# A new task order for the first attention tiles: first score ahead of the second head's similarities, first q and k in two transfers, block copies on ScalarE

## The chip, the cores and the metric

The kernel runs on one core of one Trainium2 chip. The metric is the device time of one execution in microseconds (us). A core has TensorE (PE; its weight loads are listed apart as PEld), VectorE (DVE), ScalarE (ACT), GpSimd (POOL) and SyncE (SP), which issues every transfer of this kernel.

## The reference

The kernel computes a clustered attention, then two feed-forward layers. With B = 2, H = 8 heads, S = 768 positions, D = 64 and 16 centroids per head:

```
q_assign = argmax(normalize(q) . normalize(centroids))       # and the same for k
scores   = where(q_assign == k_assign, q k^T / sqrt(D), -1e9)
attn     = softmax(scores) v                                 # 16 (batch, head) pairs
x        = attn, heads side by side                          # 1536 x 512
h        = max(x w1, x w2, x w3);  x2 = h w_out              # width 768
P        = Sinkhorn of exp(x2 w_gate), 8 rounds              # 1536 x 8
out      = sum over 8 experts e of P[:, e] * (relu(x2 w1[e]) w2[e])
```

## The kernel before

Below, a head is one of the 16 (batch, head) pairs, numbered 0 to 15, and a tile is 128 queries of a head against all its 768 keys: six tiles to a head, 96 in all, numbered g. All of the attention is written as a list of tasks. Each task has an engine, a cost in us, what it depends on, perhaps a due time, and a place (a small integer, `plan.place`). `Plan.urgency` works out, from the due times backwards, the latest moment at which each task may start. `Plan.order` adds to this moment a correction from the table `MOVES` (line 222): one number for each kind of task, a kind being the code of the task's function together with its place, numbered as they first appear. `Plan.run` then plays the list through on five queues (PE, ACT, DVE, POOL, DMA), each time taking the ready task with the smallest corrected moment. The order that comes out is the order in which the instructions are issued. On the chip each engine works through its own queue strictly in that order, and so does SP with the transfers.

All transfers that go through `dma` (line 258) share one line of code, so at each place they have one common number of `MOVES`. Before, everything of the heads' preparation stands at place 0; the tiles have place g mod 6.

- `centroids` (line 656): loads the centroids (tile csb), normalizes them (`quick_root`, lines 497 to 503), transposes them on PE (line 676, tile pt) and copies them into the tile block with two copies, one on ACT and one on DVE (lines 678 to 682).
- `norms` (line 261): loads q and k of a head in natural order (tile nat, 384 KB), squares, sums and takes the inverse norm (tile rr). For head 0 the squaring on ACT (line 276) and the sums on DVE (line 279) are done in halves, after one transfer.
- `prep` (line 298): loads q and k transposed (tile raw, 384 KB) and makes the operands of the scores: a rounded part opm (`MC_ON`, POOL, line 318) and the rests opsb and opmb (POOL, line 256 in `sub`). For head 0 the swapped halves come by a second load (tile turned, two transfers of 192 KB); for the others by copies from SBUF to SBUF, issued on SP (lines 333 to 338).
- `alone`/`sims` (lines 693 and 348): 24 small matmuls give the similarities with the centroids (tile sim), from raw and block.
- `masks` (line 361): the arg max on DVE (lines 376 to 404), then PE turns the one-hot rows (line 415 for head 0, in tile ot, 455 for the others), and they are written under the operands: for head 0 by ACT (line 427) and DVE (line 431), for the others by ACT and two transfers (line 470).
- `prep_v` (line 473): loads v of a head (tile v, 192 KB, two buffers).
- `tile_steps` (line 508): the scores of a tile (lines 521 and 524, one PSUM buffer s), a scaled copy with the row's minimum on DVE (line 535), the exponential on ACT (line 543), six transposes on PE (line 557), their copy to SBUF on ACT or DVE (line 249 or 251), and for every second tile the product with v (line 571).
- `attention` (line 688): queues head 0, then heads 1 and 2 (`AHEAD_HEADS` = 3), then the tiles; the preparation of head i + 3 is mixed in during head i.

The list `weights_first` (line 631) prepares the first weights of the layer behind the attention meanwhile. After the attention come the feed-forward layers (`moe1`, then the eight experts), which the change does not touch.

Of the kernel before, what the change touches and what calls it, by code (L numbers as in the profile page):

```python
# [13 lines left out]
AF = mybir.ActivationFunctionType  # L14
ALU = mybir.AluOpType
AX = mybir.AxisListType
# [135 lines left out]
def moe_kernel(ctx: ExitStack, tc: tile.TileContext, qk, nat, cen, wt, w123, wout, wgate, w1, w2, out):  # L152
    nc = tc.nc
# [3 lines left out]
    NQ = S // P  # L157
# [20 lines left out]
    def pool_round(dst, src):  # L178
# [39 lines left out]
    plan = Plan()  # L218
# [1 line left out]
    STEP = 2.25  # L220

    MOVES = [
# [7 lines left out]
    ]  # L230
    EARLY = 10.0
    NORM = 2
# [25 lines left out]
    def dma(fn, reads=(), writes=(), after=(), due=1e9, cost=0.65):  # L258
        return plan.task((DMA, cost), lambda e: nc.sync.dma_start(*fn()), reads, writes, after, due)

    def norms(i, gate):

        task = plan.task

        def mine(tag, shape, bufs=2, dtype=F32):
            return tile_of(a_p, tag, bufs, shape, f"{tag}{i}", dtype)

        n = mine("nat", [P, 2, NQ, D])
        dma(lambda: (n(), nat[i, :, :2]), writes=[n], cost=1.3)
        sq = n  # L270
        nqk = lambda: n().rearrange("p j t d -> p (j t) d")
        n2, y, r = (mine(t, [P, 2 * NQ]) for t in ("n2", "ry", "rr"))
        if i == 0:
            for j in range(2):
                half = lambda j=j: n()[:, j]
                done = [task((ACT, 0.45), lambda e, h=half: nc.scalar.activation(h(), h(), AF.Square), [n], (), gate)]
                task(
                    (DVE, 0.5),
                    lambda e, j=j, h=half: nc.vector.tensor_reduce(
                        n2()[:, j * NQ : (j + 1) * NQ], h(), axis=AX.X, op=ALU.add  # L280
                    ),
                    [n],
                    [n2],
                    done,
                )
            quick_root(n2, y, tile_of(ps_a, "y", 1, [P, 2 * NQ], "norm0"), r)
            return r
        if i < AHEAD_HEADS:
            task((ACT, 0.85), lambda e: nc.scalar.activation(nqk(), nqk(), AF.Square), [n], [n], gate)
        else:  # L290
            task((POOL, 2.0), lambda e: nc.gpsimd.tensor_tensor(nqk(), nqk(), nqk(), op=ALU.mult), [n], [n], gate)
        lower, upper = lambda: nqk()[:, :, : D // 2], lambda: nqk()[:, :, D // 2 :]
        task((POOL, 1.0), lambda e: nc.gpsimd.tensor_add(lower(), lower(), upper()), [sq], [sq])
        task((DVE, 0.54), lambda e: nc.vector.tensor_reduce(n2(), lower(), axis=AX.X, op=ALU.add), [sq], [n2])
        root(n2, y, r)
        return r
# [64 lines left out]
    def masks(i, r, m, free, raw, sim, mx, m2, sims, reads, due):  # L361
# [37 lines left out]
        if i == 0:  # L399

            oh = mine("oh", [P, 2, NQ, C], 2, BF16)
            task(
                small,
                lambda e: nc.vector.tensor_tensor(
                    oh().rearrange("p j t c -> p (j t) c"), w(), every(m2), op=ALU.is_equal
                ),
                [w, sim],
                [oh],
            )
            for j in range(2):  # L410
                ot = tile_of(ps_a, "t", T_BUFS, [P, 2, 512], f"ot0_{j}")

                def turn_masks(j=j, ot=ot):
                    for t in range(NQ):
                        nc.tensor.matmul(
                            ot()[D : D + C, t // 3, t % 3 * P : (t % 3 + 1) * P],
                            oh()[:, j, t],
                            ident16,
                            start=True,
                            stop=True,  # L420
                        )

                task((PE, 0.6), lambda e, f=turn_masks: f(), [oh], [ot])
                src = lambda ot=ot: ot()[D : D + C, :, :TB]
                dst = lambda j=j: m()[D : D + C, 1 - j].rearrange("p (c k) -> p c k", c=2)
                if j == 0:
                    task((ACT, 0.83), lambda e, dst=dst, src=src: nc.scalar.activation(dst(), src(), AF.Copy, scale=-BIG), [ot], [m], free)
                else:
                    task(
                        (DVE, 0.87),  # L430
                        lambda e, dst=dst, src=src: nc.vector.tensor_scalar(dst(), src(), -1.0, 1.0, op0=ALU.mult, op1=ALU.add),
                        [ot],
                        [m],
                        free,
                    )
            return reduced
# [219 lines left out]
    def centroids():  # L656

        task = plan.task
        csb, sq, n2, y, rn, cn = (
            tile_of(a_p, tag, 1, shape, f"c{t}")  # L660
            for t, tag, shape in zip(
                ("sb", "sq", "n2", "y", "r", "n"),
                ("csb", "oc", "cn2", "cy", "cr", "cn"),
                ([P, D], [P, D], [P, 1], [P, 1], [P, 1], [P, 2, D]),
            )
        )
        dma(lambda: (csb(), cen), writes=[csb], cost=0.45)
        task((ACT, 0.43), lambda e: nc.scalar.activation(sq(), csb(), AF.Square, accum_out=n2()), [csb], [sq, n2])
        quick_root(n2, y, tile_of(ps_a, "t", T_BUFS, [P, 1], "croot"), rn)
        for j in range(2):  # L670
            task((DVE, 0.16), lambda e, j=j: nc.vector.tensor_scalar(cn()[:, j], csb(), rn(), None, op0=ALU.mult), [csb, rn], [cn])
        block = cstack["block"] = plan.slot("block", 1, lambda: const.tile([P, H, 2 * C], F32, name="block"))
        task((POOL, 0.4), lambda e: nc.gpsimd.memset(block(), 0.0), [], [block])
        bank = tile_of(ps_a, "t", T_BUFS, [P, 2, 512], "pt")
        pt = lambda: bank()[:, 0]
        task((PE, 0.45), lambda e: nc.tensor.transpose(pt()[:, :P], cn().rearrange("p j d -> p (j d)"), ident), [cn], [bank])
        full = lambda: pt()[:, :P].rearrange("p (h c) -> p h c", h=H)
        for j, engine in enumerate((ACT, DVE)):
            rows, cols = slice(j * D, (j + 1) * D), slice((1 - j) * C, (2 - j) * C)
            task(  # L680
                (engine, 0.3),
                lambda e, rows=rows, cols=cols: copy(e, block()[rows, :, cols], full()[rows]),
                [bank, block],
                [block],
                shared=engine == DVE,
            )

    def attention():
        st = {}
        centroids()  # L690
        dma(lambda: (weight(), wt[:, 0]), writes=[weight])


        def alone(p):
            plan.task((PE, 0.85), lambda e: p["sims"](), p["reads"], [p["sim"]])
            return masks(**p)

        gate = [alone(prep(0, norms(0, []), []))]
        for i in range(1, AHEAD_HEADS):
            alone(prep(i, norms(i, gate), gate))  # L700
        rs = {AHEAD_HEADS: norms(AHEAD_HEADS, gate)}
        weights_first([])
        s, p = None, None
        for g in range(STEPS):
            i = g // NQ + AHEAD_HEADS
            if g % NQ == 0:
                prep_v(g // NQ)
            plan.place = g % NQ
            s = tile_steps(g, st, p if g % NQ == SIMS_AT else None)
            plan.place = 0  # L710
            if g % NQ == SIMS_AT and p:
                masks(**p)
                p = None
            if g % NQ == 0 and i < B * H:
                p = prep(i, rs.pop(i), [s])
            i += 1
            if g % NQ == NORM and i < B * H:
                rs[i] = norms(i, [s])
        return plan
# [565 lines left out]
```

## Time and profile before

| | us |
|---|---|
| median of 3 runs (lowest, highest) | 1452.43 (1452.15, 1452.87) |
| the profiled execution, its own time | 1451.71 |
| its span, first to last instruction | 1449.9 |
| PE busy in the span | 1432.6 |
| attention (up to the last product with v) | about 248 |

A row of the timeline gives the start, the duration, the engine, the line, the operation, what it writes and reads, the shape and how many instructions were merged (x24); in brackets, how long the engine had been idle and what ended that. SPq is SP's issue of a transfer, and its duration is that of the issue, not of the transfer. A landing is seen at the first instruction that waited for it.

### The profile page before, as it was taken

What the parts mean: (1) busy time and instruction counts of PE and PEld (TensorE: products, weight loads), DVE (VectorE), ACT (ScalarE), POOL (GpSimd) and SP (SyncE); (2) the same over time, 40 slices, a digit from 0 to 9 for tenths busy, and PEclk for the clock granted to TensorE, in tenths of its full rate; (3) what the DMA queues carried; (4) which work ended last, traced back from release to release, by engine and by line L of the source; (5) the groups of instructions that cost most, each with busy time, mean ns of one, the idle gap of its engine ahead of it and who ended that gap; (6) DMA issues with size and microseconds to landing.
All of it is one profiled execution on the core that took longest, in us unless ns stands there. A gap on an engine that the chain in (4) does not pass through costs nothing.

```text
span 1449.9 us, 20574 instructions
## 1 busy us (share of the span) xinstructions
PE 1432.6 (99%) x7900; PEld 1199.4 (83%) x7900; DVE 920.1 (63%) x1628; ACT 514.0 (35%) x1112; POOL 603.8 (42%) x692
## 2 busy tenths in 40 slices
PE   7999999999999999999999999999999999999999
PEld 5787777888878888888888888888888888888887
DVE  7888775455458577665655565655565655665655
ACT  6887776222125422232222222222222222222221
POOL 7676532575637433333343233343233343333320
PEclk9999999999999999999999999999999999999999
DMA  8765621112120110000111100110010110001102
GB/s 240 182 163 143 151 61 44 58 58 73 55 62 30 44 44 30 29 30 30 44 44 30 30 29 30 44 44 30 29 30 30 45 44 30 30 29 31 44 15 87
DMA packets 32066, 83.26 MB, mean 57 GB/s; under 512 B 4672, under 2 KB 9952, under 8 KB 31968
## 3 DMA queue, kind: packets, MB, share of 16 engines
q1 hardware_dynamic: 31968, 81.95, 19.7%
q8 instruction: 62, 1.02, 0.3%
q14 instruction: 36, 0.29, 0.1%
HBM read 65.46 MB, written 3.19 MB: 47 GB/s over the span
## 4 chain that ended last, share of the span: by engine, by line
PE 93%; DVE 4%; DMA 1%; POOL 1%; issue 1%; ACT 0%; SPq 0%; POOLq 0%; DVEq 0%; ACTq 0%
PE l L784 12%; PE l L785 12%; PE l L786 12%; PE y L571 4%; PE t L557 3%; PE m L784 3%; PE m L786 3%; PE m L785 3%; PE z L786 3%; PE z L784 3%; PE z L785 3%; PE y L786 3%; PE x L786 3%; PE y L785 3%; PE x L785 3%; PE y L784 3%
## 5 line engine op out<-in xcount | busy, mean ns | idle before, releaser
L1191 DVE SCALAR_TENSOR_TENSOR acc<-l,prob,acc 128x512 f32<-128x512 f32 (+1 forms) x337 | 251.6, 747 | 125.5 <-PE l L786 122.5
L784 PE MATMUL l<-w,h 128*128 128x512 f32 (+1 forms) x770 | 302.5, 393 | 0.0
L785 PE MATMUL l<-w,h 128*128 128x512 f32 (+1 forms) x770 | 301.5, 392 | 0.0
L786 PE MATMUL l<-w,h 128*128 128x512 f32 (+1 forms) x770 | 299.2, 389 | 0.0
L1123 ACT ACTIVATE h<-c 128x512 fp32r<-128x512 f32 (+1 forms) x186 | 98.0, 527 | 368.4 <-DVE c L1152 190.6
L941 POOL TENSOR_TENSOR wop_t<-ts,wop_t 128x256 fp32r<-128x256 f32 x124 | 91.3, 747 | 245.7 <-ACT wop_t L940 245.7
L941 POOL TENSOR_TENSOR wop_b<-wraw,wop_b 128x256 fp32r<-128x256 f32 x97 | 79.0, 815 | 266.7 <-ACT wop_b L940 266.7
L1124 DVE SCALAR_TENSOR_TENSOR h<-c,h 128x512 fp32r<-128x512 f32 (+1 forms) x186 | 112.8, 606 | 110.4 <-ACT h L1123 110.4
L786 PEld LDWEIGHTS l<-w,h 128*128 128x128 f32 x770 | 144.7, 188 | 31.5
L784 PEld LDWEIGHTS l<-w,h 128*128 128x128 f32 x770 | 145.4, 189 | 24.4
L785 PEld LDWEIGHTS l<-w,h 128*128 128x128 f32 x770 | 145.4, 189 | 22.6
L951 POOL TENSOR_TENSOR w<-wraw,w 128x512 fp32r<-128x512 f32 x64 | 82.6, 1292 | 96.8 <-ACT w L950 96.8
L535 DVE TENSOR_SCALAR_CACHE_REDUCE e<-s 128x768 f32<-128x768 f32 x96 | 91.7, 955 | 33.9 <-PE s L524 30.9
L543 ACT ACTIVATE e<-e,nm 128x768 f32<-128x768 f32 x96 | 90.3, 940 | 30.9 <-DVE e L535 30.4
L1123 ACT ACTIVATE h<-x 128x512 fp32r<-128x512 f32 (+1 forms) x62 | 30.6, 493 | 188.2 <-PE x L786 188.2
L784 PE MATMUL m<-x,mhi 128*128 128x512 f32 x216 | 84.4, 391 | 0.0
L786 PE MATMUL m<-x,mhi 128*128 128x512 f32 x216 | 84.0, 389 | 0.0
L785 PE MATMUL m<-x,mlo 128*128 128x512 f32 x216 | 84.0, 389 | 0.0
L786 PE MATMUL x<-x,wop_b 128*128 128x512 f32 (+1 forms) x248 | 83.3, 336 | 0.0
L786 PE MATMUL y<-s,wop_t 128*128 128x512 f32 (+1 forms) x248 | 83.3, 336 | 0.0
L785 PE MATMUL y<-s,wop_t 128*128 128x512 f32 (+1 forms) x248 | 83.3, 336 | 0.0
L785 PE MATMUL x<-x,wop_b 128*128 128x512 f32 (+1 forms) x248 | 83.3, 336 | 0.0
(201 smaller groups left out, 3024.1 us busy)
## 6 DMA issues: line engine op xcount, KB each, us to landing
wraw<-in_w SPq DMA_DIRECT2D x64, 512.0 KB, 4.0
mraw<-in_w SPq DMA_DIRECT2D x18, 512.0 KB, 3.6
nat<-in_nat SPq DMA_DIRECT2D x16, 384.0 KB, 4.4
raw<-in_qk SPq DMA_DIRECT2D x16, 384.0 KB, 4.4
v<-in_nat SPq DMA_DIRECT2D x16, 192.0 KB, 4.4
r<-row SPq DMA_DIRECT2D x16, 192.0 KB, 4.0
mraw<-in_wout SPq DMA_DIRECT2D x8, 384.0 KB, 3.1
opsb<-opm SPq DMA_DIRECT2D x15, 192.0 KB, 4.1
```

Source lines behind the costliest of these rows:

```text
L535: lambda e: nc.vector.tensor_scalar(ex(), scores(), -SCALE, None, op0=ALU.mult, op1=ALU.min, accum_out=nm()),
L543: lambda e: nc.scalar.activation(ex(), ex(), AF.Exp, bias=nm(), scale=-1.0, accum_out=sm()[:, n]),
L557: nc.tensor.transpose(t()[:, c, ks], ex()[:, c, ks], ident)
L571: nc.tensor.matmul(y()[c * D : (c + 1) * D], v()[:, c * (NQ // 2) + k], at()[:, :, c, k * P : (k + 1) * P], start=k == 0, stop=k == NQ // ...
L784: nc.tensor.matmul(ps, whi, xlo, start=first, stop=False, skip_group_check=more)
L785: nc.tensor.matmul(ps, wlo, xhi, start=False, stop=False, skip_group_check=more)
L786: nc.tensor.matmul(ps, whi, xhi, start=False, stop=last, skip_group_check=more)
L941: nc.gpsimd.tensor_sub(w[:, 1], src[key], f32(w[:, 0]))
L951: nc.gpsimd.tensor_sub(w[:, 1], raw[:, j], f32(w[:, 0]))
L1123: nc.scalar.activation(h[:, :, 0], z, AF.Relu)
L1124: nc.vector.scalar_tensor_tensor(h[:, :, 1], z, 0.0, f32(h[:, :, 0]), op0=ALU.max, op1=ALU.subtract)
L1191: nc.vector.scalar_tensor_tensor(a, l2, prob[:, tt, e : e + 1], a, op0=ALU.mult, op1=ALU.add)
```

## The change

Head 0's preparation gets a place of its own (-1), and so do that of head 1 (-2) and head 2 (-3), so `MOVES` has 155 numbers in place of 96, all of them new. The first q and k come in two transfers, and each half is squared and summed as it lands. The two copies into block are both on ACT. v of head 0 is queued with head 0's preparation, and the first tile's scores are queued before heads 1 and 2, whose similarities must come after these scores. The cost in the plan of the similarities that run alone is 1.5 in place of 0.85, that of turning the masks 0.75 in place of 0.6.

```diff
     MOVES = [
-        -1820.61, 299.75, 22.5, 59.09, 0, 45.73, -175.17, 207.12, -429.98, -75.94, -770.87, 163.46, -19.3,
...
+        -3443.95, -535.85, 242.61, -3.55, 30.49, 0, -76.34, -801.5, 0, 105.65, 5.02, 80.19, 0, -403.58, 600.2,
+        -369.75, 0, 246.57, -0.32, 36.71, 0, 0, -1.72, -533.66, 3.8, -203.93, -618.01, 15.75, -54.98, 0,
+        -5.83, 48.86, 117.7, -17.18, -550.1, 0, -281.52, 0, 0, -826.3, 7655.22, 76.09, 50.25, -2.01, 141.05,
+        -990.4, 380.05, 112.34, -95.83, 321.65, 294.95, 61.4, 30.17, -8.69, -52.92, 149.36, 92.27, -281.93,
+        49.6, -0.08, -983.11, 0.74, -5.04, 67.19, 44.86, 822.3, -6.95, 253.69, 70.19, -502.9, 917.43, -19.84,
...
     ]
         n = mine("nat", [P, 2, NQ, D])
-        dma(lambda: (n(), nat[i, :, :2]), writes=[n], cost=1.3)
+        if i > 0:
+            dma(lambda: (n(), nat[i, :, :2]), writes=[n], cost=1.3)
...
         if i == 0:
             for j in range(2):
                 half = lambda j=j: n()[:, j]
-                done = [task((ACT, 0.45), lambda e, h=half: nc.scalar.activation(h(), h(), AF.Square), [n], (), gate)]
-                task(
-                    (DVE, 0.5),
...
+                done = [dma(lambda j=j, h=half: (h(), nat[i, :, j]))]
+                done = [task((ACT, 0.47), lambda e, h=half: nc.scalar.activation(h(), h(), AF.Square), after=done)]
+                done = [
+                    task(
+                        (DVE, 0.52),
...
+                        writes=[n2],
+                        after=done,
+                    )
+                ]
+                n.users.extend(done)
...
-        for j, engine in enumerate((ACT, DVE)):
+        for j, engine in enumerate((ACT, ACT)):
...
-        def alone(p):
-            plan.task((PE, 0.85), lambda e: p["sims"](), p["reads"], [p["sim"]])
+        def alone(p, after=()):
+            plan.task((PE, 1.5), lambda e: p["sims"](), p["reads"], [p["sim"]], after)
             return masks(**p)
 
+        plan.place = -1
         gate = [alone(prep(0, norms(0, []), []))]
+        prep_v(0)
+        plan.place = 0
+        first = tile_steps(0, st, None)
         for i in range(1, AHEAD_HEADS):
-            alone(prep(i, norms(i, gate), gate))
+            plan.place = -1 - i
+            alone(prep(i, norms(i, gate), gate), [first])
+        plan.place = 0
         rs = {AHEAD_HEADS: norms(AHEAD_HEADS, gate)}
...
-            if g % NQ == 0:
+            if g and g % NQ == 0:
                 prep_v(g // NQ)
             plan.place = g % NQ
-            s = tile_steps(g, st, p if g % NQ == SIMS_AT else None)
+            s = tile_steps(g, st, p if g % NQ == SIMS_AT else None) if g else first
```

## Rows read from the trace of the kernel before

**Rows 1.** The page's busy time of each engine: us, share of the span, instructions.

```profile
PE 1432.6 (99%) x7900; PEld 1199.4 (83%) x7900; DVE 920.1 (63%) x1628; ACT 514.0 (35%) x1112; POOL 603.8 (42%) x692
```

**Rows 2.** Waits of PE, 0 to 250 us: us in total, times, longest.

```profile
PE pt L676 <- DVE cn L671: 5.1, 1, 5.1
```

**Rows 3.** The chain of work that ended last, some products with v: start, us.

```profile
24.88 1.45 PE y L571 x12
...
41.48 1.45 PE y L571 x12
...
65.50 1.45 PE y L571 x12
...
79.47 1.45 PE y L571 x12
...
107.37 1.45 PE y L571 x12
...
122.63 1.45 PE y L571 x12
```

**Rows 4.** Timeline 0 to 40 us, SP's issues of the first transfers.

```profile
1.19 0.42 SPq L259 DMA_DIRECT2D nat<-in_nat  x1
...
1.65 0.43 SPq L259 DMA_DIRECT2D raw<-in_qk  x1
2.12 1.20 SPq L259 DMA_DIRECT2D turned<-in_qk  x2
...
3.36 0.59 SPq L259 DMA_DIRECT2D wt_sb<-in_wt  x1
...
6.73 0.92 SPq L259 DMA_DIRECT2D v<-in_nat  x2
```

**Rows 5.** Timeline 0 to 40 us, the engines up to the second tile's scores.

```profile
4.77 0.94 ACT L276 ACTIVATE nat<-nat 128x384 f32<-128x384 f32 x2 [1.26 <-DMA nat<-in_nat]
...
6.35 0.83 POOL L179 TENSOR_SCALAR opm<-raw 128x768 fp32r<-128x768 f32 x1 [4.62 <-DMA raw<-in_qk]
...
6.72 1.49 PE L351 MATMUL sim<-block,raw 128*64 128x32 f32 x24 [1.15 <-DVE block L251]
...
9.94 1.80 POOL L256 TENSOR_TENSOR opmb<-raw,opm 64x768 fp32r<-64x768 f32 x1
...
10.65 1.45 PE L415 MATMUL ot<-ident,oh 128*16 128x128 bf16 x12 [2.44 <-DVE oh L404]
...
12.03 1.50 PE L351 MATMUL sim<-block,raw 128*64 128x32 f32 x24
12.13 0.80 ACT L427 ACTIVATE opm<-ot 16x768 fp32r<-16x768 f32 x1 [0.70 <-PE ot L415]
...
13.45 1.01 PE L521 MATMUL s<-opmb,opsb 128*128 128x384 f32 x2
...
14.26 0.84 PE L524 MATMUL s<-opm 80*128 80x384 f32 x2
...
16.02 0.23 DVE L490 RECIPROCAL rr<-rr 128x12 f32<-128x12 f32 x1
...
16.16 1.01 PE L521 MATMUL s<-opmb,opsb 128*128 128x384 f32 x2 [1.06 <-DVE e L535]
```

**Rows 6.** Timeline 0 to 40 us, six transposes before and after the clock rose.

```profile
17.61 1.48 PE L557 MATMUL t<-ident,e 128*128 128x128 f32 x6
...
20.91 0.88 PE L557 MATMUL t<-ident,e 128*128 128x128 f32 x6 [0.18 <-ACT e L543]
```

**Rows 7.** Timeline 0 to 40 us, head 1: its mask rows' transfers, its first tile's scores.

```profile
22.80 1.65 SPq L259 DMA_DIRECT2D opm<-oc  x1
...
29.37 0.51 PE L524 MATMUL s<-opm 80*128 80x384 f32 x2
```

**Rows 8.** Transfers by line: count, KB each, median us from issue to landing.

```profile
opm<-oc SPq DMA_DIRECT2D x30, 48.0 KB, 2.7
...
csb<-in_cen SPq DMA_DIRECT2D x1, 32.0 KB, 1.8
```

More of the change, by code (lines that the diff above doesn't have):

```diff
@@ L275, in norms @@
                 half = lambda j=j: n()[:, j]
-                done = [task((ACT, 0.45), lambda e, h=half: nc.scalar.activation(h(), h(), AF.Square), [n], (), gate)]
-                task(
-                    (DVE, 0.5),
[L279 to L285, printed above, removed]
+                done = [dma(lambda j=j, h=half: (h(), nat[i, :, j]))]
[3 more added lines that the diff above has]
+                        (DVE, 0.52),
+                        lambda e, j=j, h=half: nc.vector.tensor_reduce(
+                            n2()[:, j * NQ : (j + 1) * NQ], h(), axis=AX.X, op=ALU.add
+                        ),
+                        writes=[n2],
[3 more added lines that the diff above has]
+                n.users.extend(done)
             quick_root(n2, y, tile_of(ps_a, "y", 1, [P, 2 * NQ], "norm0"), r)
@@ L421, in turn_masks @@
                         )
-                task((PE, 0.6), lambda e, f=turn_masks: f(), [oh], [ot])
+                task((PE, 0.75), lambda e, f=turn_masks: f(), [oh], [ot])
                 src = lambda ot=ot: ot()[D : D + C, :, :TB]
```

13 rows, old and new, of the table MOVES are left out of this document.

## The prediction

> **What bounds the kernel now.** I read the busy times first: PE works 1432.6 us of a span of 1449.9 [rows 1], so 17.3 us of the span are without PE work, and only these, and what PE does at its lower clock, can be won by a new order. The waits of PE come next: 5.1 us pass before its first instruction [rows 2], and the rest of the large waits lie in the first 17 us [rows 5]. The reader is to see there the start as a race of three chains towards the first score: the centroids to block, the norms and the arg max to the turned masks, and raw through POOL to opmb. Last, the chain that ended last tells how regular the 96 tiles run: from 65.50 to 79.47 three pairs of tiles, one head's worth, take 13.97 us [rows 3]. Three pairs take 16.60 us from 24.88 to 41.48, and 15.26 from 107.37 to 122.63: 2.6 and 1.3 us over the even pitch. So the attention holds some 3.9 us of hitches after its start. The expert layers behind it are not touched. About 0.2%, 2.9 us, is what a measurement of this kernel can tell from no change.
>
> The sum is made against the profiled execution, 1451.71 us (span 1449.9 and 1.8 around it); it is 0.7 below the median of the runs, and I carry the difference over to the median 1452.43.
>
> **The change part by part.**
>
> *Similarities of head 1 behind the first scores.* Before, PE turns the masks until 12.10, then does head 1's 24 similarities (12.03, 1.50 us), and only at 13.45 the first scores, which end at 15.10. Then it is idle 1.06 us until DVE has emptied the only score buffer, and the second scores start at 16.16 [rows 5]. With the exchange the similarities lie in that gap: scores 1.65 us, similarities 1.5, second scores. If nothing else held the first scores, they would end at 12.10 + 1.65 = 13.75 and the second would start at 13.75 + 1.5 = 15.25, or 0.9 earlier. Most it can be worth is the gap, 1.06. The first scores also need opmb, which POOL finishes at 9.94 + 1.80 = 11.74, and the mask rows, which ACT finishes at 12.93 [rows 5]: line 521 alone may run before the latter. Both are just in time, by 0.4 us and by nothing. Head 1's masks lose nothing by the later similarities: its inverse norms are ready only at 16.25 [rows 5], and the similarities would end by about 15.3 to 16.2.
>
> *The new order of SP's queue.* This is the term that I count against it. All transfers of place 0 share one number of the table, now -3443.95, while head 0's own have -403.58, head 1's -2.01 and head 2's -6.95 (numbers 0, 13, 43 and 66, counting kinds as they appear). Due times within the attention differ by some 250 us at most, so a place-0 transfer that is ready goes before all of head 0's. Ready at the start are three: csb, the small weight table wt and v of head 1, which has a second buffer and stays at place 0. So SP would issue csb, wt, v of head 1, then q, k, raw, turned twice, v of head 0. Before, nat was issued at 1.19, raw at 1.65, wt at 3.36, and both v at 6.73 [rows 4]. What is put ahead of nat costs SP 0.59 for wt and about 0.45 for a v (0.92 for two), 1.04 us together [rows 4]. From below: the transfers run behind one another, raw landing at 6.35 where nat had landed at 4.77, 384 KB in 1.58 us [rows 5]; v's 192 KB are half of that, 0.8 us, and if wt's 0.59 were hidden wholly in the transfers, that is all. If the first bytes are faster than this pair shows, it may be 0.5. From above: the splitting of nat adds one more issue, 0.45, ahead of raw, so 1.5. I take 1.0 for raw, nearest to the issue rows, and keep 0.5 to 1.5.
>
> Then raw lands at 7.35. POOL works from raw to opmb without a pause worth naming, 5.39 us (6.35 to 11.74), so opmb is ready at 12.75. The similarities of head 0 cannot start before raw: 7.35 in place of 6.72, and the turned masks end 0.63 later, at 12.73. ACT's mask rows follow 0.83 later, at 13.56. The first scores run 12.8 to 14.4 or so, the similarities of head 1 to 15.9, and the second scores start near 16.0 in place of 16.16. So the gain of 0.9 shrinks to 0.2; with raw 0.5 later it is 0.65, with 1.5 it is a loss of 0.3.
>
> *q and k in two transfers.* The first half lands about 0.8 us before the second, half of 1.58, and ACT and DVE treat it meanwhile; the second half's squaring and sum are then all that follows its landing, some 0.5 us saved. But both halves lie behind wt and v, so k lands at about 4.77 + 1.04 = 5.8. From nat's landing to the turning of the masks it was 5.88 us (4.77 to 10.65) [rows 5]; 0.5 less makes 5.4 and a turning at 11.2, where raw's chain gives 10.65 + 0.63 = 11.28. So I cost the splitting at nothing; the cover is raw's later landing. If raw were not late, it would be worth up to the 0.4 us by which DVE's sums end earlier. By the Trainium skill, "DMA: Bandwidth & Descriptors", section "Anatomy of one DMA", a transfer has a fixed cost of about 2 us, and the section "Bandwidth" asks for large transfers, which speaks against splitting. Worked out as an estimate from that figure, k would land 2 us later, and the sum would be about 1454. Here the rows differ: raw was issued 0.46 us behind nat and landed 1.58 behind it, so the fixed parts overlap [rows 4, 5].
>
> *Both block copies on ACT.* DVE's copy came late behind the sums and released the similarities at 6.72, though raw was there at 6.35 [rows 5]. On ACT the second copy would be done by about 6.2: at most 0.4 us. With raw at 7.35 it is worth nothing, for the same cover.
>
> *The rest of the 155 numbers.* They reorder DVE, ACT, POOL and SP through all of the attention. PE bounds the even stretches at 13.97 us a head, so a new order there can only win back hitches (3.9 us at most) or add some of the same size. Between these ends I take zero, as the even pitch, which most heads show, is the nearest row. The clock is a second open term: six transposes take 1.48 us at 17.61 and 0.88 at 20.91, where PE goes on at the higher of its two levels (2.4 for 1.2 GHz) after 10 us of work with gaps [rows 6]. With the gap of 1.06 filled it may rise earlier. I do not count that, but each us of it is worth about half a us.
>
> Sum: exchange -0.9, late raw +0.7, the others 0: -0.2 against the profile, 1451.5, so 1452.2 as a median.
>
> **The rivals.**
>
> 1. *The early part works as its words say*: wt and v of head 1 cost nothing, because they hide in the first transfers' latency. Then 0.9 for the exchange, 0.4 for block, and perhaps 0.5 of clock: 1450.6. For it: csb's 32 KB take 1.8 us to land, mostly latency [rows 8]. Against it: raw landed a full transfer behind nat.
> 2. *The new order also takes hitches out*: of the 3.9 us, and with the first 0.9, it wins 3 to 4.5, so about 1448.6. For it: the two hitches stand at definite spots [rows 3]. Against it: no row tells that the new numbers touch them.
> 3. *Slower: head 1 waits for its operands.* Place-0 transfers (nat and raw of head 3, then v of head 2) now go before head 1's and head 2's copies and mask rows on SP. Before, the last mask rows of head 1 were issued at 22.80, 1.65 us long, and landed by about 22.80 + 1.65 + 2.7 = 27.2, while the first scores that need them ran at 29.37: 2.2 us of slack [rows 7, 8]. One transfer of 384 KB put in between takes 1.58 us and is hidden. Two take 3.2 and cost 1.0, and a place-0 transfer that itself waits in the queue for a free buffer adds its wait. It decides from a delay of 2.2 us on; with two large transfers and a buffer wait of about 3, for two heads, it costs some 4 us: 1456.2.
> 4. *The halves of nat run one after the other*, not overlapped: k then lands later by about the time of a small transfer, 1.8 us [rows 8], at 7.6; with 5.4 us from there the masks are turned at 13.0 in place of 11.28, so the sum is 1.7 higher: 1453.9. The row of raw behind nat speaks against it. The rule of the Trainium skill cited above would have it so.
>
> **How the numbers follow.** The forecast, no change within 0.2% with a small gain, has 0.42. Rival 1 has 0.15 and rival 4 has 0.05; both also lie within 0.2%. Rival 2 has 0.22, rival 3 has 0.16. So: faster 0.22, same 0.62, slower 0.16. The range reaches down to 1448.2, which leaves a third of rival 2 out, and up to 1456.0, which leaves about half of rival 3 out; the forecast's own range, from the price of the late raw (-0.65 to +0.3) and a hitch more or less (1.3), is 1450.5 to 1453.8.
>
> **What would show it.** In the changed kernel's timeline SP should issue wt and a v before nat, and raw should be taken up by POOL at about 7.3. PE should do the scores of the first tile, then 24 similarities, then scores without the 1.06 us of idle time. Raw at 6.4 would make rival 1 right. The three pairs from the first product with v on should take about 16.6 us; under 15 speaks for rival 2. A wait of PE for the operands opm or opsb at the seventh or thirteenth tile's scores would be rival 3. A squaring of k after 6.5 us would be rival 4. The prediction is wrong if the first product with v comes at about the same time, and the total still moves by over 2.9 us: then the order of the later heads decides.

## The result and the profile after

The changed kernel takes 1459.91 us, median of 6 runs (1457.68 to 1462.05), against 1452.28 for the kernel before (6 runs, 1452.06 to 1452.87): a ratio of 1.0052, 95% interval 1.0042 to 1.0063. So it is slower by 7.6 us, and the prediction of 1452.2, with a range to 1456.0, missed it. The profiled execution took 1459.87, its span is 1458.1, 8.2 over that of before.

The page's busy times after, to be set against [rows 1]:

```profile
PE 1434.1 (98%) x7900; PEld 1199.0 (82%) x7900; DVE 920.0 (63%) x1627; ACT 512.3 (35%) x1113; POOL 602.5 (41%) x692
```

PE does the same 7900 matmuls. It is busy 1.5 us longer and idle 24.0 us in place of 17.3, so 6.7 of the 8.2 us are new idle time. The next view says where. It is the table by stretches of 25 us; its columns are the stretch, its length, then busy time and instructions of PE, PEld, DVE, ACT and POOL, the granted clock, the share of the DMA engines and GB/s. First before:

```profile
0.00:25.00 25.00, 15.06 (x127) 12.70 (x129) 15.26 (x42) 15.29 (x32) 17.81 (x29) 1.00 0.80 243
25.00:50.00 25.00, 24.01 (x213) 18.99 (x211) 21.89 (x53) 19.05 (x43) 17.03 (x21) 1.00 0.88 226
50.00:75.00 25.00, 25.00 (x207) 19.93 (x206) 21.92 (x50) 21.61 (x45) 17.52 (x21) 1.00 0.56 146
75.00:100.00 25.00, 25.00 (x224) 20.05 (x220) 21.70 (x49) 20.23 (x42) 19.34 (x24) 1.00 0.70 181
100.00:125.00 25.00, 24.00 (x217) 19.32 (x215) 21.50 (x45) 20.02 (x44) 11.98 (x15) 1.00 0.67 162
```

and after:

```profile
0.00:25.00 25.00, 12.94 (x91) 10.67 (x93) 12.70 (x38) 13.76 (x28) 15.24 (x25) 1.00 0.81 236
25.00:50.00 25.00, 21.95 (x196) 17.12 (x193) 20.89 (x50) 17.34 (x41) 18.57 (x23) 1.00 0.80 191
50.00:75.00 25.00, 23.87 (x218) 19.23 (x216) 22.12 (x46) 20.18 (x44) 13.94 (x17) 1.00 0.69 184
75.00:100.00 25.00, 23.64 (x211) 18.74 (x210) 21.11 (x46) 18.89 (x42) 16.49 (x21) 1.00 0.53 135
100.00:125.00 25.00, 24.59 (x201) 19.24 (x200) 21.01 (x48) 20.16 (x44) 18.92 (x23) 1.00 0.52 139
```

PE's idle time (25.00 less the first busy figure) grows by 2.1 us in the first stretch, 2.1 in the second, 1.1 in the third and 1.4 in the fourth, and shrinks by 0.6 in the fifth: 6.1 of the 6.7. So the start is one quarter of the loss, and most of it falls in the three stretches behind. Behind 125 us the idle time grows by another 0.6.

**The start.** The timeline after, 0 to 25 us, against [rows 4 to 6]:

```profile
1.18 0.42 SPq L264 DMA_DIRECT2D wt_sb<-in_wt  x1
...
1.64 0.43 SPq L264 DMA_DIRECT2D v<-in_nat  x1
2.11 0.91 SPq L264 DMA_DIRECT2D nat<-in_nat  x2
...
3.06 0.43 SPq L264 DMA_DIRECT2D raw<-in_qk  x1
...
4.79 0.52 ACT L283 ACTIVATE nat<-nat 128x384 f32<-128x384 f32 x1 [1.40 <-DMA nat<-in_nat]
...
8.20 0.52 ACT L283 ACTIVATE nat<-nat 128x384 f32<-128x384 f32 x1 [2.89 <-DMA nat<-in_nat]
...
9.78 0.83 POOL L179 TENSOR_SCALAR opm<-raw 128x768 fp32r<-128x768 f32 x1 [8.05 <-DMA raw<-in_qk]
...
9.84 1.50 PE L360 MATMUL sim<-block,raw 128*64 128x32 f32 x24 [4.40 <-DMA raw<-in_qk]
...
13.45 1.85 POOL L261 TENSOR_TENSOR opmb<-raw,opm 64x768 fp32r<-64x768 f32 x1
13.75 1.45 PE L424 MATMUL ot<-ident,oh 128*16 128x128 bf16 x12 [2.42 <-DVE oh L413]
...
15.35 1.01 PE L530 MATMUL s<-opmb,opsb 128*128 128x384 f32 x2 [0.15 <-POOL opmb L261]
...
17.03 1.50 PE L360 MATMUL sim<-block,raw 128*64 128x32 f32 x24
...
18.46 1.01 PE L530 MATMUL s<-opmb,opsb 128*128 128x384 f32 x2
...
24.78 1.51 PE L580 MATMUL y<-at,v 128*64 128x256 f32 x12
```

SP issues in the order foretold: wt and a v ahead of both halves of nat, raw behind them. PE does scores, similarities, scores, and the 1.06 us of idle time are gone. But raw is taken up at 9.78 in place of 6.35, 3.4 us later. POOL's chain to opmb is about as long as before (9.78 to 15.30, 5.5 us against 5.4), so the first scores wait for it until 15.35, 1.9 later than at 13.45; without the exchange, which takes 1.5 us of similarities from ahead of them, it would have been some 3.1, an estimate from the masks, which are turned at 13.75 in place of 10.65. The second half of nat landed 3.4 us behind the first. The first product with v starts at 24.78, where it started at 24.81 in the same view (24.88 in the chain of [rows 3]); yet this is no sign of a start without loss, since PE's queue now has it behind the fourth tile's scores, and before it stood behind the fifth's.

**The later heads.** The timeline after, 24 to 125 us, some rows with PE's new idle time and what stands before them on DVE and POOL:

```profile
26.49 0.46 SPq L264 DMA_DIRECT2D opmb<-opm  x1
...
27.63 1.44 SPq L264 DMA_DIRECT2D opm<-oc  x2
...
32.08 0.58 PE L530 MATMUL s<-opmb,opsb 128*128 128x384 f32 x2 [1.14 <-DVE w L398]
...
49.59 0.88 PE L566 MATMUL t<-ident,e 128*128 128x128 f32 x6 [1.11 <-ACT e L552]
...
60.79 0.83 POOL L179 TENSOR_SCALAR opm<-raw 128x768 fp32r<-128x768 f32 x1 [3.10 <-PE s L533]
...
60.94 0.95 DVE L544 TENSOR_SCALAR_CACHE_REDUCE e<-s 128x768 f32<-128x768 f32 x1
...
61.71 1.85 POOL L261 TENSOR_TENSOR opmb<-raw,opm 128x768 fp32r<-128x768 f32 x1
...
61.93 1.91 DVE L781 TENSOR_SCALAR ta<-ta 128x512 int32<-128x512 int32 x1
...
63.87 0.69 DVE L783 SCALAR_TENSOR_TENSOR ta<-mraw,ta 128x512 int32<-128x512 int32 x1
...
64.48 0.95 DVE L544 TENSOR_SCALAR_CACHE_REDUCE e<-s 128x768 f32<-128x768 f32 x1
...
65.50 0.61 PE L530 MATMUL s<-opmb,opsb 128*128 128x384 f32 x2 [1.13 <-DVE e L544]
...
72.91 1.29 POOL L791 TENSOR_TENSOR ta<-ta,mhi 128x512 f32<-128x512 f32 x1
73.23 1.52 DVE L789 SCALAR_TENSOR_TENSOR ta<-mraw,ta 128x512 f32<-128x512 uint32 x1
...
75.68 0.62 PE L530 MATMUL s<-opmb,opsb 128*128 128x384 f32 x2 [0.42 <-DVE e L544]
...
95.25 0.62 PE L530 MATMUL s<-opmb,opsb 128*128 128x384 f32 x2 [0.94 <-DVE e L544]
```

Three kinds of gap are to be seen. At 32.08 the scores of head 1's first tile (the seventh tile) wait 1.14 us; the DVE operation named as releaser makes nothing that these scores read. What line 530 does read is opmb, and head 1's copy opmb from opm was issued at 26.49, where the kernel before issued it at 22.21. The mask rows, which line 533 reads right behind, were issued at 27.63, 4.8 later than in [rows 7]. At 49.59 transposes wait 1.11 us for an exponential, which on ACT stood behind copies of mask rows into oc. At 65.50, 75.68, 95.25 and, in the same way, 105.45 the scores wait 1.13, 0.42, 0.94 and 0.41 us for DVE's copy that empties s, and DVE was held there by pieces of `weights_first`: two in a row ahead of 65.50 and of 95.25, one ahead of 75.68 and of 105.45. A piece of 0.36 or 0.69 us took 1.91 and 1.52 where POOL had just begun an operation. Together with two of 0.40 these gaps are 5.95 us. The kernel before has 1.85 from 24 to 125 us: 0.45 at the seventh tile, 0.40, and 1.00 at the 44th tile. Its trace reads:

```profile
28.94 0.59 PE L521 MATMUL s<-opmb,opsb 128*128 128x384 f32 x2 [0.45 <-issue]
...
112.85 1.83 POOL L256 TENSOR_TENSOR opmb<-raw,opm 128x768 fp32r<-128x768 f32 x1
...
113.07 2.17 DVE L768 SCALAR_TENSOR_TENSOR ta<-mraw,ta 128x512 int32<-128x512 int32 x1
...
116.62 0.62 PE L521 MATMUL s<-opmb,opsb 128*128 128x384 f32 x2 [1.00 <-DVE e L535]
```

So these gaps grew by 4.1 us. Over the whole span PE's idle time behind 25 us grew by 4.6 (11.9 in place of 7.4). With the start's 2.1 and PE's 1.5 of longer busy time that makes the 8.2.

### The profile page after: what moved, and what is told of

It reads as the page before. It is cut to its first block, busy times and chain, and to the rows that moved or that the text cites. A ratio compares the mean times of both kernels' runs of the same rounds, so it can differ in the third digit from the quotient of the medians.

```text
span 1458.1 us, 20596 instructions
## 1 busy us (share of the span) xinstructions
PE 1434.1 (98%) x7900; PEld 1199.0 (82%) x7900; DVE 920.0 (63%) x1627; ACT 512.3 (35%) x1113; POOL 602.5 (41%) x692
## 3 DMA queue, kind: packets, MB, share of 16 engines
q8 instruction: 62, 1.02, 0.3%
## 4 chain that ended last, share of the span: by engine, by line
PE 89%; DVE 5%; DMA 2%; POOL 2%; issue 1%; ACT 1%; SPq 1%; POOLq 0%; DVEq 0%; ACTq 0%
PE l L799 12%; PE l L800 12%; PE l L801 12%; PE z L801 3%; PE z L799 3%; PE z L800 3%; PE m L799 3%; PE m L800 3%; PE m L801 3%; PE y L580 3%; PE y L801 3%; PE x L801 3%; PE y L800 3%; PE x L800 3%; PE y L799 3%; PE x L799 3%
```

## The experiments

In the diffs, `behind(a, b)` puts task a directly behind task b in the finished order, and `queues[E]` is the order of one engine, from which the list is merged again. Every ratio is to the kernel before on the same chip.

**The start's two transfers, each undone alone.** In the changed kernel: wt and head 1's v back behind head 0's transfers, q and k in one transfer, both; and wt and v put ahead in the kernel before.

```diff
 # a1_wt_v_behind, a3_both (changed kernel)
+    behind("wt", "turned1")
+    behind("v1", "raw1")
 # a2_one_nat, a3_both (changed kernel): one transfer in place of two
+    plan.tasks[mark["q"]] = (*whole[:2], lambda e: nc.sync.dma_start(mark["n"](), nat[0, :, :2]), *whole[3:])
+    tasks.pop(at("k"))
 # b1_wt_v_ahead (kernel before): wt and v of head 1 directly behind csb
```

> The changed kernel with two transfers moved on SP's queue and nothing else: wt behind the second turned, v of head 1 behind raw of head 1. Theory T (the first transfers): raw lands at 7 to 8 us in place of 9.78, the first scores start 2 us sooner, and with the lateness its followers at the heads 1 to 6 go too: 1452 to 1454. Theory N (the new numbers' order of the engines and of SP later on): the start gains 2 us, the steps at tiles 6 to 35 stay (about 6 us): 1457 to 1458.

> The changed kernel with q and k of head 0 in one transfer at the place of q; wt and v of head 1 stay ahead. If it is the halves that make k and raw late (k landed 3.4 us behind q), raw lands near 8 and the time falls by 1 to 4 us, to 1456 to 1459. If wt and v ahead do it, k lands at about 6 with q, raw stays near 9.5, and the time stays within 1 us of the changed kernel's 1459.9.

> The changed kernel with both: one transfer for q and k, wt behind turned, v of head 1 behind raw of head 1. The first transfers then go out as before. Theory T: raw lands at 6.3, the first scores end near 13.8, and the whole is at 1451 to 1453. Theory N: the start is as good, but the steps at tiles 6 to 35 stay: 1456 to 1458.

> The kernel before with wt and v of head 1 issued directly behind csb, and nothing else. Theory T: raw lands at 7.5 to 9, the start is 1 to 2.5 us late and steps at heads 1 to 6 follow: 1454 to 1459. Theory N: it costs what the start loses at most: 1453 to 1454.5.

The times at which POOL takes up raw and PE starts the first scores, from the timelines, and the medians:

```
                    raw     first scores   median us   ratio (95%)
kernel before       6.35    13.45
a3  neither         6.17    11.88          1457.35     1.0039 (1.0027 to 1.0052)
a1  split alone     7.24    12.81          1458.48     1.0043 (1.0030 to 1.0056)
a2  wt, v alone     8.47    13.96          1460.24     1.0055 (1.0042 to 1.0067)
changed kernel      9.78    15.35          1459.91     1.0052 (1.0042 to 1.0063)
b1  before + wt, v  8.57    15.34          1453.58     1.0013 (1.0004 to 1.0022)
```

Both parts delay raw, and they add up: wt and v by 2.2 to 2.5 (b1 against before, a2 against a3, the changed kernel against a1), the split by 1.1 (a1 against a3) to 1.3 (the changed kernel against a2). Each time is that of one execution, and raw's landing varies: with the first transfers as before it is taken up between 5.56 and 6.49 in the twelve profiles taken, with wt and v ahead and no split between 8.28 and 8.57 in three. So the part of wt and v is clear, and that of the split is good to about half a us. In b1 the delay comes through to the total: every tile is 1.9 to 2.0 later, and so is the median, 1453.58 against 1451.67 (interval 0.6 to 3.2). In the changed kernel it does not wholly: a3's first scores are 3.5 us earlier, but its loss against before is 5.7 us in place of 7.6. And with first scores 1.6 us ahead of before's, a3 is still slower by those 5.7. Hence the start is the smaller part: theory N's ranges hold for a3 and b1, theory T's do not. And the seventh tile takes back some of what a faster start gives. The medians of a1 and a2 cannot price the two transfers, as both kernels lose 3.7 us at the 14th and 15th tiles, where a3 loses 0.3 and the changed kernel 0.7. In a3's timeline, PE:

```profile
28.77 0.59 PE L533 MATMUL s<-opmb,opsb 128*128 128x384 f32 x2 [1.76 <-DMA opmb<-opm]
```

The row of 32.08 again, waiting 1.76 in place of 1.14, and here the releaser is head 1's copy opmb from opm.

**The exchange alone, and with the copies.** In the kernel before, head 1's similarities behind the first scores on PE (b2), and the second copy into block on ACT as well (b3).

```diff
 # b2, b3
+    q = queues[PE]
+    q.remove(mark["sims1"])
+    q.insert(q.index(mark["score0"]) + 1, mark["sims1"])
 # b3
+    queues[DVE].remove(mark["copy1"])
+    queues[ACT].insert(queues[ACT].index(mark["copy0"]) + 1, mark["copy1"])
```

> The kernel before with one exchange on PE: head 1's similarities behind the first tile's scores. The prediction's term: the second scores start 0.9 us earlier, 1450.5 to 1451.5 (0.9 below the kernel before, within 0.3 where a later wait takes it back).

> The same exchange, and both block copies on ACT. Head 0's similarities start at about 6.35 (raw) in place of 6.72, so the masks are turned 0.3 us sooner; the first scores still wait for opmb at 11.74. Together 1.0 to 1.3 below the kernel before: 1450.2 to 1451.

b2 took 1451.18 (0.9995, 0.9987 to 1.0004), b3 1451.61 (0.9996, 0.9988 to 1.0005), the kernel before 1452.14. In the profiles the second tile's scores come 0.7 us earlier in b2 and 1.0 in b3. In b3 all later tiles keep that; in b2, whose profiled execution (1453.03) is its slowest, 2.4 us are lost again up to the 26th tile. So by the start's rows the exchange is worth 0.7, and the copies up to 0.3 where raw is not late (in b3 raw itself came early, at 5.56). The medians, whose intervals reach over 1, cannot tell either from no change.

**SP's order against the engines' order.** The changed kernel with the order of transfers of before (c1), the kernel before with the new order of transfers (c2).

```diff
 # c1 (changed kernel, one transfer for q and k), c2 (kernel before)
+    queues[DMA] = [...]
+    tasks = merge(plan, queues, tasks)
```

> The changed kernel with every transfer on SP in the order of the kernel before (and one transfer for q and k); PE, ACT, DVE and POOL keep the new order. Theory Q (the new order of SP's queue: transfers of later heads go before head 1's copies, so PE waits for head 1's operands): the steps at tiles 6 to 35 vanish, 1450 to 1452. Theory E (the new order of the engines makes the steps): as with the first transfers alone restored, 1456 to 1458.

> The kernel before with every transfer on SP in the order of the changed kernel (one transfer for q and k stays); the engines keep the order of before. Theory Q: the 2 us of wt and v ahead and the steps on top, 1457 to 1460. Theory E: only the 2 us of the late start, 1453 to 1455.

c1 took 1464.92 (1.0091, 1.0077 to 1.0104) and c2 1477.57 (1.0181, 1.0167 to 1.0195). Neither half carries the loss by itself: an order of transfers fits the engines' order it was made with, and either with the other is worse than both whole. In c1's profile 8.8 us are lost at one tile, the ninth, a delay that neither kernel has. This experiment could not attribute the loss, and that is its result.

**The later order alone.** f1 is the changed kernel with a3's transfers, whose order is new up to the fourth tile's scores and that of before behind them; f2 is the kernel before up to the thirteenth tile's scores, with the new order behind.

```diff
+    rest = [...]
+    tasks = tasks[:100] + [(0.0, i) for i in rest]   # f1; f2 cuts at the thirteenth tile
```

> The changed kernel, first transfers as before, new order up to the scores of the fourth tile, and behind them everything in the order of the kernel before. If the loss lies in the order of the later heads: the start's gain of 0.9 and a hitch or two where the orders meet, 1451 to 1453. If the new order of the first tiles brings it (head 1's operands late from the start on): a step of 2 us at tile 6 and more behind it, 1455 to 1458.

> The kernel before up to the scores of the thirteenth tile, and behind them everything in the order of the changed kernel. If the loss lies in the later heads: steps at tiles 19, 23, 31, 35 and behind tile 91, the one at 43 gone, together 4 to 5 us: 1456 to 1457. If it comes from the first tiles: within 1.5 us of the kernel before.

f2 took 1455.47 (1.0025, 1.0015 to 1.0034), 3.9 us over the 1451.61 of before (interval 2.2 to 4.9), with a start like before's; its span is 2.8 longer. Its timeline has the same gaps as the changed kernel, at the same tiles:

```profile
56.98 1.83 POOL L257 TENSOR_TENSOR opmb<-raw,opm 128x768 fp32r<-128x768 f32 x1
...
57.20 1.89 DVE L768 TENSOR_SCALAR ta<-ta 128x512 int32<-128x512 int32 x1
...
60.74 0.62 PE L522 MATMUL s<-opmb,opsb 128*128 128x384 f32 x2 [1.10 <-DVE e L537]
```

1.10 here, then 0.41, 0.90 and 0.41, where the changed kernel has 1.13, 0.42, 0.94 and 0.41; the 1.00 us of before at the 44th tile are gone. So the new order of the heads behind the second costs some 3 to 4 us without any part of the start. Added up as an estimate, this 3.9 and b1's 1.9 are 5.8 of the 7.6 us. f1 took 1454.72 (1.0018, 1.0009 to 1.0027), but its loss sits at the seam: the fifth and sixth tiles lose 2.9 and 1.9 us against before, as the old order does not find head 1 as far as it was. It says nothing of the start's worth.

**The two causes behind the start, undone one at a time.** d1 is a3 with the weight pieces behind the same tasks as before; d2 is a3 with head 1's copies ahead of the loads of head 3 on SP; d3 has both; d4 is the kernel before with the weight pieces where the new order has them.

```diff
 # d1, d3 (a3), d4 (before)
+    queues[ACT] = [...]
+    queues[DVE] = [...]
+    queues[POOL] = [...]
 # d2, d3 (a3): opsb<-opm and opm<-opm of head 1 ahead of nat of head 3, opsb<-opmb ahead of its raw
+    queues[DMA] = [...]
```

> The changed kernel with the first transfers of before (as in the run with both restored), and the pieces of the first weights on ACT, DVE and POOL queued behind the same tasks as in the kernel before. Theory W (two weight pieces in a row on DVE ahead of a tile's copy make the steps at tiles 19, 23, 31 and 35, 1.4 + 0.8 + 1.2 + 0.8 us): those steps go, the step of before at tile 43 (1.2) comes back, so about 3 us less than with the weights as changed (1457.35): 1454 to 1455. Theory S (later heads still follow from SP's order): the steps stay within 0.5 us, 1457.

> The same start, and on SP head 1's copies ahead of nat of heads 3 and 4 and of raw of head 3; nothing else. Theory Q, for tile 6 alone: PE's wait for head 1's operands (1.76 us there) shrinks to under 0.7: 1456 to 1456.5. If the wait comes from the engines' order before the copies, it stays, 1457.3.

> Both of these. If the two are independent, their gains add: 1453 to 1454. What is left against the kernel before plus the exchange (1451.2) is then from the rest of the new order.

> The kernel before with only the weight pieces on ACT, DVE and POOL queued where the changed kernel has them. Theory W: steps at tiles 19, 23, 31 and 35 of some 4 us together, the step at 43 gone: 1454.5 to 1455.5. Theory S: within 0.7 us of the kernel before.

They took 1458.9 (1.0049, 1.0037 to 1.0061), 1459.71 (1.0050, 1.0037 to 1.0063), 1459.4 (1.0051, 1.0039 to 1.0063) and 1455.21 (1.0023, 1.0015 to 1.0032), against 1451.85 before. The weight pieces are confirmed as a cause: d4 alone makes the kernel before 3.4 us slower, most of f2's 3.9, with steps of 1.9 us at the 20th and the 31st tile. In d1 the gaps at 65.50 and 95.25 are gone, while the 24th and 36th tiles (75.68 and 105.45) still lose 0.8 and 0.5. In d2 the gap at 32.08 is gone. But nothing is won, and d1, d2 and d3 all miss what was expected of them. d1 has new delays of 0.5 to 1.7 us at seven other tiles (the twelfth, 14th, 18th, 40th, 42nd, 48th and 54th). In d2 the tile behind head 2's first comes 2.2 us later, and its timeline says why:

```profile
41.06 0.61 SPq L277 DMA_DIRECT2D opm<-oc  x1
...
44.70 0.27 ACT L483 ACTIVATE oc<-ot 96x128 fp32r<-96x128 bf16 x1 [3.48 <-DMA opm<-oc]
44.73 0.58 PE L548 MATMUL s<-opm 80*128 80x384 f32 x2 [0.91 <-DMA opm<-oc]
...
46.80 0.88 PE L582 MATMUL t<-ident,e 128*128 128x128 f32 x6 [1.49 <-ACT e L568]
```

Head 2's last mask rows, issued at 41.06, land some 3.6 us later. PE's scores wait for them 0.91 us, and so does ACT, which stands 3.48 us before its next copy into oc, with an exponential behind it for which PE then waits 1.49. So the wait for operands moved from head 1 to head 2. But this happens without d2's edit too: in a1, a2 and d1, whose copies stand as in a3, PE waits only 0.25, 0.49 and 0.23 us at the seventh tile, and then 1.51, 1.48 and 1.48 for the same exponential. That the order of head 1's copies makes the gap at 32.08 is therefore argued from the rows and not shown. A cause can be right and its removal worth nothing while the neighbours' order was made around it.

**A kernel from what was learnt.** e1 is b3 with one weight piece of DVE moved away from POOL's operation at 112.85, and the piece of ACT that needs it moved with it.

```diff
+    for piece, engine, other in (("piece2_2", DVE, "sum37"), ("piece2_3", ACT, "exp42")):
+        q = queues[engine]
+        q.remove(mark[piece])
+        q.insert(q.index(mark[other]) + 1, mark[piece])
```

> The kernel before with the exchange and both copies on ACT, and the one weight piece that takes 2.17 us at 113 us moved on DVE behind the next sum (and the ACT piece that follows it behind the next exponential). The exchange gives 1.1, the step at tile 43 1.3: 1449.5 to 1450.5, the fastest of all; if the piece collides with POOL again at its new place, 1451.

e1 took 1449.8 (1448.93 to 1451.03), 0.9986 with an interval of 0.9977 to 0.9995, against 1451.61: 1.8 us, faster than both kernels, though by less than 0.2%. Its timeline around the moved piece:

```profile
111.99 1.83 POOL L269 TENSOR_TENSOR opmb<-raw,opm 128x768 fp32r<-128x768 f32 x1
...
114.71 0.67 DVE L783 SCALAR_TENSOR_TENSOR ta<-mraw,ta 128x512 int32<-128x512 int32 x1
```

Begun after POOL's end (113.82) the piece takes 0.67 in place of 2.17, and the gap of 1.00 us at the 44th tile is gone: that tile gains 1.2 on those before it.

## Why the prediction was wrong, point by point

*What bounds.* Right: all that moved is PE's idle time, at the start and in definite hitches; the expert layers took no part.

*The exchange, -0.9, and the copies on ACT.* Right in mechanism, and near in size: 0.7 and up to 0.3 by the profiles of b2 and b3. In the changed kernel raw hides the copies, as foretold, and the exchange still takes 1.5 us of similarities out of the way of the first scores.

*SP's new order, raw 1.0 us later.* Order and mechanism right, size wrong. The term was worked out from the issue times (0.59 and 0.45) and from 384 KB in 1.58 us. Measured alone it is 2.2 for raw and 1.9 for the total (b1), beyond the upper bound of 1.5. The step that failed is "v's 192 KB are half of that, 0.8 us": how long the transfers took when queued together was read from a pair at the head of the queue. In b1 nat is squared at 5.36, only 0.6 later than before; it is the distance from nat to raw that grew, from 1.58 us to 3.21, and the prediction had carried that over unchanged.

*q and k in two transfers, nothing.* Wrong. "The cover is raw's later landing" overlooked that raw stands behind both halves in the same queue: the split delays the cover itself, by 1.1 to 1.3 us. Rival 4's mark was seen as well: k was squared at 8.20, after 6.5, and the masks turned at 13.75, where that rival had 13.0. But its reason, halves that do not overlap by nature, does not hold: in a1, with only csb ahead of them, the halves are squared at 3.61 and 4.35, 0.74 apart (ACT did not wait for the first, so it may have landed sooner). The fixed cost of about 2 us by the Trainium skill, "DMA: Bandwidth & Descriptors", section "Anatomy of one DMA", which the prediction weighed, is given there for transfers that GpSimd issues, and here SP issues them; a second such cost is not seen between the two halves of a1. What the 3.4 us are in the changed kernel depends on what was queued ahead.

*The rest of the 155 numbers, zero.* This is the step that decided. "Between these ends I take zero, as the even pitch, which most heads show, is the nearest row": the even pitch shows what a good order gives, and is no evidence that another order of the same work gives it too. PE's idle time behind 25 us grew by 4.6 us, over the upper end of 3.9. That 3.9 was itself read too high as something to win back: PE is idle only 0.6 us of the 16.60 and 1.0 of the 15.26, and the rest by which these exceed the even pitch is PE's work. By itself the new order behind the thirteenth tile costs 2.8 in the span and 3.9 in the median (f2). Of rival 2, one piece came true: the hitch at the 44th tile went.

*Rival 3.* Its mark was seen: the place-0 loads of head 3 go before head 1's copies, the mask rows are issued 4.8 us later, more than the 2.2 of slack, and the seventh tile waits. In d2, where the copies go first, that wait is gone, but in d1, where they do not, it is 0.23 us, so the mechanism is likely and not shown. Its price of 4 us for two heads was too high: 1.14 us in the changed kernel, and 1.76 in a3, whose start is earlier. Near 49.59 it is an exponential that PE waits for. ACT had stood idle 1.95 us in front of its next copy into oc. In d2 the same copy waits for the transfer out of oc, and in the changed kernel that transfer was issued at 44.01, 3.5 us before ACT went on at 47.49; that this is the same wait was read from the rows, not tested.

*The sum.* The start came out with 2.1 us more of idle time where the forecast had a gain of 0.2; the later heads cost 4.6 where it had 0. The second alone brings the time past the end of the range (1452.2 + 4.6 = 1456.8), and with the first it lies far outside. The cases were priced one at a time, and a slow start together with a bad later order was none of them. The prediction's last sign came true: the first product with v starts at the same time and the total still moves by over 2.9 us. The order of the later heads did decide, but the equal start is half luck, as PE now does that product one tile earlier.

*What stays open.* Of the 1.5 us by which PE is busy longer, 1.0 is in the transposes of the exponentials (73.2 us before, 74.2 after, by line); which of them was not traced. Neither was the reason why the transfers at the head of the queue take longer together than one by one.

## What to carry to other kernels

When a planner's numbers are all replaced, price the new order of every queue as a term of its own, with a loss as likely as a gain; a table of delays tile by tile finds where it went. Ahead of the first load that the start waits for, look at every transfer that is issued: a small table and 192 KB together, not tried apart, delayed raw by 2.2 us here. Split a load only if what follows it in the queue can wait. Before a piece of other work is put into a gap of one engine, look what the engine it shares a path with does in that gap.

## What the runs showed of the hardware that was not expected

**DVE stands while POOL works, in some pairs.** Each of the long pieces of weights begins 0.2 to 0.9 us after POOL began an operation, and ends 0.3 to 0.6 us after POOL's end: 61.93 to 63.84 against 61.71 to 63.56, 73.23 to 74.75 against 72.91 to 74.20, 113.07 to 115.24 against 112.85 to 114.68 in the kernel before. Moved behind POOL's end the last one took 0.67 (e1). DVE's copy out of s (0.95) runs beside POOL at its usual length, as in the row of 60.94 to 61.89 beside POOL's operation from 60.79. In the kernel before one piece of DVE begins first, at 42.40, and takes its usual 0.69; there it is POOL's operation of 1.83, begun at 42.48, that takes 2.29. The Trainium skill, "SBUF — State Buffer", section "Who interferes with whom", has this as a rule: an operation of DVE with two inputs in SBUF, or one with a single input in a fast mode, and one of GpSimd that reads SBUF lock each other out, whichever came first, for the whole instruction. These rows agree. The rule would have been a reason to look at which POOL operation each moved piece lands beside.

**Transfers queued together at the start.** The stretch from 5 to 10 us, before and then after (columns as above):

```profile
5.00:10.00 5.00, 1.94 (x25) 1.54 (x25) 3.91 (x13) 3.94 (x8) 3.49 (x4) 1.00 1.02 333
```

```profile
5.00:10.00 5.00, 0.60 (x5) 0.34 (x6) 1.18 (x3) 1.75 (x6) 0.22 (x1) 1.00 0.97 231
```

The DMA engines are as busy (1.02 and 0.97) but move 231 GB/s in place of 333. The second half of q and k, 192 KB, is squared 0.74 us behind the first with only csb ahead of both (a1), and 3.4 us behind it with wt and a v ahead as well.

**The pace of PE and the granted clock.** The granted clock stands at 1.00 in the first 25 us of both kernels, while six transposes take 1.48 us early and 0.88 later [rows 6]. In the changed kernel six transposes take 1.16 us at 22.61, and scores first take 0.62 us at 23.87; before, the pace had risen by 20.91. The prediction held an earlier rise possible; it came 2 to 3 us later.

```profile
22.61 1.16 PE L566 MATMUL t<-ident,e 128*128 128x128 f32 x6
...
23.87 0.62 PE L530 MATMUL s<-opmb,opsb 128*128 128x384 f32 x2
```
